# Chunks of 512 tokens from token 6016 on instead of 7424, with the last two transforms in fewer steps and one plain pair instead of two

## The chip, the core and the metric

The kernel runs on one core of one Trainium2 chip. The metric is the device time of one execution in microseconds. The core has five engines that work side by side and wait for each other by semaphores: TensorE (PE in the profile; its weight loads, which overlap the matmuls, are PEld), VectorE (DVE), ScalarE (ACT), GpSimd (POOL) and SyncE (SP), which here only issues DMAs. PE writes its results to PSUM, and DVE and ACT read them from there.

## The reference, cut to what matters

A spectral mixing of `x` (4 batches of 3008 tokens by 256) is followed by a two-layer network of width 2048 over all 12032 tokens.

```python
def _attn_ref(x, w_r, w_i, b_r, b_i):
    X = np.fft.rfft(x, axis=1)
    Yr = Xr @ w_r - Xi @ w_i + b_r
    Yi = Xr @ w_i + Xi @ w_r + b_i
    Yr = np.sign(Yr) * np.maximum(np.abs(Yr) - lam, 0.0)   # lam = 0.01, and the same for Yi
    y = np.fft.irfft(Y, n=x.shape[1], axis=1)

def _moe_ref(x, w_in, w_out, alpha):
    h = x @ w_in
    g = np.maximum(h, 0.0) + alpha * np.minimum(h, 0.0)
    return g @ w_out
```

All is float32. The kernel keeps the accuracy with products of numbers split into a high and a low part: three matmuls (high x high, high x low, low x high) stand for one product.

## The kernel before

**The transforms.** Each batch of 3008 = 47 x 64 tokens goes through these parts. Part a (`a_load`, `a_split`, `a_mm`, `a_evac`) is the first stage of the forward transform, in 16 groups g, whose results are stored to DRAM. Part b (`b_load`, `b_mm`, `b_evac`, `b_evac2`), part m (`m_mm`, `m_mm2`, `m_part`, `m_evac1`: the mixing with `w_r`, `w_i`, the bias and the threshold) and part c (`c_mm`, `c_evac`, with a second store to DRAM) work through 12 slots q; together they are called the middle part here. Part d (`d_load` and `d_step`, or `s_dmm` and `s_dpart`) is the last stage of the inverse transform: each of its 32 runs (dg, 8 to a batch) makes 376 tokens, in PSUM, from which ACT and DVE write the high and low parts `yh`, `yl` that the network reads. The parts take their PSUM tiles from one pool of three, `ps_f`, in the order in which they ask.

**The network.** The tokens go through in chunks. Up to token `T0` a chunk has 384 tokens (256 for chunks 0 and 16), and one *step* is one of the 16 blocks of 128 hidden columns: `l1_step` does 6 matmuls of the first layer into a tile of `ps_h` (two tiles, L680), ACT and DVE make the activation (L686, L687) and split it (L691, L692, the low part on DVE or POOL), and three steps later `l2_step` does the second layer, 9 matmuls of 256 columns (6 in a 256-token chunk; L717 to L719). From `T0` on, a chunk has 512 tokens and one *pair* t of 0 to 7 is two of the 16 blocks: `s_l1` does 12 matmuls of 512 columns (L784), with ACT's L787 and DVE's L788 as activation; `s_sums` makes the operands for the second layer; `s_l2` does that two pairs later. It takes the pair as a 2 x 2 block product, by Winograd's form with seven block products of 3 matmuls (21 matmuls of 256 columns, L884 to L886) where `t` is not in `PLAIN`, and by eight (24 matmuls) where it is. For the form with seven, `s_sums` also makes the differences `t13`, `t24` (t in the profile; L815, L817, L819) and splits them (L820 to L823, the last on POOL); for a plain pair it splits one half-block instead (L806, L808). Both write `dh`, `dl` (L803 with L818 or L807). At the end of a chunk `s_out` (L909 to L919) adds the products up, two pairs into the next chunk, and `s_turn` (L928) transposes the result and stores it, two pairs later, behind `s_sums` of pair 3. The last of the 512-token chunks is done plainly (`z_parts`, L830 and L831, and `z_l2`, L847 to L849: 24 matmuls a pair), with its output written from `zo` tiles.

**The order of the work** is written out by hand. The list of steps has `NS` entries (16 per chunk, 20 chunks, so 320). The functions of the transforms are hung on step numbers with `at(i, fn, ...)`: what stands in `todo` is issued after the matmuls of step i, what stands in `mid` in the middle of it. `AO[b]` is the step at which part a of batch b begins (group g at `AO + 3g//2`), `BO[b]` that of slot 0 of the middle part, and `BP` the number of steps between two slots; slot q of batch 1 is at 49 + 11q//2. Within a slot that begins at step i, m follows at i + 2 and i + 4 and c at i + 8. The d part of a chunk that begins at step i is issued at i - 3. The last 26 steps also make the combined weights of the seven-product form (`w_open`, `w_full`, `w_sums`, `w_split`), in the place of the tables of parts b and c. In the 512-token stage the d parts hang on pairs (`pre`, `post`). Every engine runs its instructions in the order of issue. Most loads and stores are issued from SP's queue, in that order.

The values of the plan that the change touches (L953 to L957):

```python
    AO = {2: 120, 3: 186}
    BO = {2: 154, 3: 222}
    BP = 5
    SLAG = 2
    PLAIN = (1, 2)
```

Of the kernel before, what the change touches and what calls it, by code (L numbers as in the profile page):

```python
# [9 lines left out]
F32 = mybir.dt.float32  # L10
F32R = mybir.dt.float32r
# [4 lines left out]
AF = mybir.ActivationFunctionType  # L16
# [77 lines left out]
def fft_mix_moe(ctx, tc, x, w_r, w_i, b_r, b_i, w_in, w_out, alpha, la, rb, lc, rd, lf, cf, sel, out):  # L94
    nc = tc.nc
    B, S, C = x.shape
    DFF = alpha.shape[0]
    CT = C // 128
    FT = DFF // 128
# [6 lines left out]
    NC = 2 * NCH  # L106
    TC = 384
    assert NC * TC - 128 == NC * TOK

    CC = 20  # L110
    SC = 512

    def head(c):
        return 128 - (TC - TOK) * (c % NC) if c % NC else 0

    def size(c):
        return TC if c % NC else TC - 128

    T0 = (CC // NC) * NC * TOK + TC * (CC % NC) - (128 if CC % NC else 0)
    NS2 = (B * S - T0) // SC  # L120
    assert CC % NC and T0 + SC * NS2 == B * S
    NPAIR = NSLOT // 2

    const = ctx.enter_context(tc.tile_pool(name="const", bufs=1))
    work = ctx.enter_context(tc.tile_pool(name="work", bufs=2))
    dram = ctx.enter_context(tc.tile_pool(name="dram", bufs=4, space=bass.MemoryType.DRAM))
    ps_f = ctx.enter_context(tc.tile_pool(name="ps_f", bufs=3, space=bass.MemoryType.PSUM))
    ps_h = ctx.enter_context(tc.tile_pool(name="ps_h", bufs=2, space=bass.MemoryType.PSUM))
    ps_o = ctx.enter_context(tc.tile_pool(name="ps_o", bufs=2, space=bass.MemoryType.PSUM))

    V, G, A, PE = nc.vector, nc.gpsimd, nc.scalar, nc.tensor

    def f(t):
        return t.bitcast(F32)
# [27 lines left out]
    FH = FT // 2  # L162
    x_s = const.tile([NP, R, C], F32, tag="half0", name="x0")
    a0_s = const.tile([NQ, R // 2, 2, C], F32, tag="half1", name="a0")
    wi_h, wo_h = {}, {}
# [166 lines left out]
    def put(*queues):  # L332
        for n, (o, i) in enumerate(stores):
            (queues or (nc.sync,))[n % max(len(queues), 1)].dma_start(out=o, in_=i)
        stores.clear()

    xt = {}
# [240 lines left out]
    def d_open(c):  # L578
# [3 lines left out]
        if head(c):  # L582
            for t, src in zip((hi, lo), heads.pop(c)):
                if c < CC:
                    t, src = t[:, :, 0:head(c)], f(src)[:, :, 0:head(c)]
# [8 lines left out]
    def d_step(b, g):  # L594
        t = zt.pop((b, g))
        c = NCH * b + g
        assert c < CC
        n0 = (size(c) - head(c)) // CH
# [20 lines left out]
    def s_open(n):  # L619
        yt[CC + n] = [work.tile([128, CT, SC], F32R, tag=tag, name=tag) for tag in ("yh", "yl")]  # L620

    def s_parts(dg):

        s, e = TOK * dg, TOK * dg + TOK
        for n in range((s - T0) // SC, (e - 1 - T0) // SC + 1):
            a, z = max(s, T0 + SC * n), min(e, T0 + SC * (n + 1))
            yield n, (a - s) // CH, (z - s) // CH, a - T0 - SC * n, z - T0 - SC * n

# [6 lines left out]
    def s_dpart(dg, n):  # L635
        parts = []
        for k, n0, n1, a, z in s_parts(dg):
            if k == n:
                for ct in range(CT):
                    ps = ds[dg][ct][:, :, n0:n1]  # L640
                    ys = [y[:, ct] for y in yt[CC + n]]
                    if n == NS2 - 1:
                        hi, lo = (y[:, a:z].rearrange("p (n i) -> p n i", i=CH) for y in ys)
                        parts.append((ps.rearrange("p i n -> p n i"), hi, lo))
                    else:
                        parts.extend(s_dput(ps, ys, a // CH, z // CH))
        for src, hi, lo in parts:
            A.activation(out=hi, in_=src, func=AF.Copy)
        for src, hi, lo in parts:
            V.tensor_tensor(out=lo, in0=src, in1=f(hi), op=ALU.subtract)  # L650
# [84 lines left out]
    PR = FT // 2  # L735
# [37 lines left out]
    sg, sa, sq = {}, {}, {}  # L773

    def s_l1(n, t):
        yh, yl = yt[CC + n]
        q = work.tile([128, 2, SC], F32, tag="xt", name="sq")
        for j in range(2):
            m = 2 * t + j
            ps = ps_h.tile([128, SC], F32, tag="h", name="ps_h")  # L780
            k = 0
            for ct in range(CT):
                for w, a in ((0, yh), (0, yl), (1, yh)):
                    PE.matmul(ps, wi_h[m // FH][:, w, ct, 128 * (m % FH):128 * (m % FH) + 128], a[:, ct],  # L784
                              start=(k == 0), stop=(k == 3 * CT - 1))
                    k += 1
            A.activation(out=q[:, j], in_=ps, func=AF.Relu, scale=-1.0)  # L787
            V.scalar_tensor_tensor(out=q[:, j], in0=q[:, j], scalar=beta_s[:, m:m + 1], in1=ps,  # L788
                                   op0=ALU.mult, op1=ALU.add)
        sq[n, t] = q  # L790

    def s_sums(n, t):
        q = sq.pop((n, t))
        if n == NS2 - 1:
            z_parts(t, q)
            return
# [7 lines left out]
        d = [(dh[:, HS * k:HS * k + HS], dl[:, HS * k:HS * k + HS]) for k in range(3)]  # L804
        if t in PLAIN:
            A.activation(out=h13[:, 0], in_=b12, func=AF.Copy)  # L806
# [19 lines left out]
    def z_parts(t, q):  # L826
        g = []
        for j, tags in enumerate((("xh", "Yh"), ("xl", "Yl"))):
            hi, lo = (work.tile([128, SC], F32R, tag=tag, name="zg") for tag in tags)
            A.activation(out=hi, in_=q[:, j], func=AF.Copy)  # L830
            (V if j else G).tensor_tensor(out=lo, in0=q[:, j], in1=f(hi), op=ALU.subtract)  # L831
            g.append((hi, lo))
        sg[NS2 - 1, t] = g

    def z_l2(t):
        n = NS2 - 1
        if t == 0:
            sa[n] = [ps_f.tile([128, 2, C], F32, tag="f", name="ps_o") for _ in range(2)]
        g = sg.pop((n, t))
        for i in range(4):  # L840
            o = sa[n][i // 2][:, i % 2]
            cols = slice(128 * i, 128 * i + 128)
            for j, (hi, lo) in enumerate(g):
                m = 2 * t + j
                w = wo_h[m // FH][:, m % FH]
                last = m == FT - 1 and i % 2 == 1
                PE.matmul(o, hi[:, cols], w[:, 0], start=(m == 0 and i % 2 == 0), stop=False)  # L847
                PE.matmul(o, hi[:, cols], w[:, 1], start=False, stop=False)
                PE.matmul(o, lo[:, cols], w[:, 0], start=False, stop=last)  # L849
            if t == PR - 1 and i % 2:  # L850
                for k in (i - 1, i):
                    st = work.tile([128, C], F32, tag="gh", name="zo", bufs=4)
                    if k % 2 == 0:
                        A.activation(out=st, in_=sa[n][i // 2][:, 0], func=AF.Copy)
                    else:
                        V.tensor_copy(out=st, in_=o)
                    z_store(T0 + SC * n + 128 * k, st)
                put(nc.sync, nc.scalar)

    def z_store(s0, st):  # L860

        s = s0
        while s < s0 + 128:
            d = s // TOK
            e = min(s0 + 128, (d + 1) * TOK)
            dst = out.rearrange("(b p r) c -> b p r c", b=B, r=R)[d // NCH][:, CH * (d % NCH):CH * (d % NCH) + CH]
            stores.append((dst[(s - d * TOK) // CH:(e - d * TOK) // CH], st[s - s0:e - s0]))
            s = e

    def s_l2(n, t):  # L870
# [16 lines left out]

        if t in PLAIN:
            b11, b22, b21, b12 = sg.pop((n, t))
# [60 lines left out]
    ES = [1, 1, 1, 1, 1, 1, 1, 1, 1, 0, 1, 0, 0, 0, 0, 0]  # L950
    LOS = [0, 1, 0, 0, 1, 1, 0, 1, 1, 0, 1, 1, 0, 1, 0, 0, 1, 1, 0, 0, 1, 0, 1, 1, 1, 1, 1, 0, 1, 1, 0, 1, 1, 0, 1, 1, 0, 1, 1, 0, 1, 1, 0, 1, 1, 0, 1, 1]
    DS = 3
    AO = {2: 120, 3: 186}  # L953
    BO = {2: 154, 3: 222}
    BP = 5
    SLAG = 2
    PLAIN = (1, 2)  # L957
    MP = [3, 4, 4, 4, 4, 5, 5, 6]
    CM = 8
    PB = 49  # L960
# [20 lines left out]
    with tc.manual_schedule():  # L981
# [100 lines left out]
        def at(i, fn, *args, when=todo):  # L1082
            when.setdefault(i, []).append((fn, args))
# [9 lines left out]
        for b in range(B):  # L1093
            s0 = b * per
            for g in range(J if b == 0 else 0, min(NCH, CC - NCH * b)):
                i = s0 + g * FT
# [6 lines left out]
            if b == 0:  # L1103
                for g in range(FILL, NG):
                    i = 6 * (g - FILL) + 9
# [4 lines left out]
            else:  # L1110
                for g in range(NG if b + 1 < B else 0):
                    i = AO[b + 1] + 3 * g // 2
                    if g % 2 == 0:
# [4 lines left out]
            for q in range(NPAIR if b + 1 < B else 0):  # L1118
                i = PB + 11 * q // 2 if b == 0 else BO[b + 1] + BP * q
                at(i - BL, b_load, b + 1, q)  # L1120
# [11 lines left out]
        done = 0  # L1132
        spairs = [(n, t) for n in range(NS2) for t in range(PR)]
        pre, post = {}, {}
        i = NS - 26
# [54 lines left out]
        for k in range(len(spairs) + SLAG):  # L1190
            do(pre, k)
            if k < len(spairs):
                s_l1(*spairs[k])
            do(post, k)
            put()
            if k < SLAG:
                l2(NS - 2 + 2 * k)
            if k == 1:
                do(todo, NS - 1)
            if k >= SLAG:  # L1200
                n, t = spairs[k - SLAG]
                if n == NS2 - 1:
                    z_l2(t)
                else:
                    s_l2(n, t)
                    if t == PR - 1:
                        s_out(n)
            if k < len(spairs):
                s_sums(*spairs[k])
            if k >= SLAG and t == 1 and n:  # L1210
                s_turn(n - 1)
# [33 lines left out]
```

## Time and profile before

| | |
|---|---|
| median of 3 runs | 1384.43 us |
| the runs | 1384.43, 1385.01, 1381.59 us |
| the profiled execution | 1381.03 us, span 1379.1 us, mean granted TensorE clock 0.998 |
| PE busy | 1363.7 us, 99% of the span |
| DVE, ACT, POOL busy | 927.3, 735.7, 398.2 us |
| the 384-token stage, steps 0 to 319 | 107 to 967 us |
| the eight 512-token chunks in the form with seven products | 967 to 1324 us |
| the last chunk of 512 tokens | 1324 to 1374 us |

The span is the time from the first to the last instruction of the profiled execution. Matmuls are pipelined, and their ends in the profile are modelled: one of 256 columns is shown as 0.28 us long, while the next one begins 0.12 us after it. So PE's busy share says little by itself, and lengths are read from start to start.

### The profile page before, as it was taken

How to read it: one execution, taken by the hardware profiler on the slowest of the kernel's cores; microseconds unless marked ns; L12 is line 12 of the kernel's file. 1: busy time of each engine (PE TensorE's matmuls, PEld its weight loads, DVE VectorE, ACT ScalarE, POOL GpSimd, SP SyncE). 2: the span in 40 equal slices, each digit the busy share in tenths (PEclk: the TensorE clock that was granted, in tenths of full speed). 3: DMA queues.
4: the chain of work that ended last, by engine and by line, in shares of the span. 5: the costliest groups of instructions: out<-in, count | busy, mean ns of one | idle time of the engine just before them, and what ended most of it. 6: DMA issues, size and time to landing. Idle time of an engine off the chain costs nothing.

```text
span 1379.1 us, 25262 instructions
## 1 busy us (share of the span) xinstructions
PE 1363.7 (99%) x9550; PEld 1295.2 (94%) x9550; DVE 927.3 (67%) x1689; ACT 735.7 (53%) x1519; POOL 398.2 (29%) x432
## 2 busy tenths in 40 slices
PE   9999999999999999999999999999999999999998
PEld 5979899999999999999999999999999999999997
DVE  2757755666665546676657667666788888888874
ACT  3565655544556645556545454555555555555553
POOL 4855822322322123322222223222112111111121
PEclk9999999999999999999999999999999999999999
DMA  9964222102113311134212111101101110111001
GB/s 239 255 184 148 64 92 73 54 25 62 57 55 107 87 47 54 36 116 132 65 50 62 54 43 58 43 23 36 35 1 39 27 28 5 36 27 28 9 9 31
DMA packets 77700, 89.66 MB, mean 65 GB/s; under 512 B 28829, under 2 KB 60032, under 8 KB 77579
## 3 DMA queue, kind: packets, MB, share of 16 engines
q1 hardware_dynamic: 68993, 76.74, 19.2%
q0 software_dynamic: 5168, 8.02, 2.2%
q10 hardware_dynamic: 3418, 3.29, 0.7%
q8 instruction: 75, 1.23, 0.4%
q14 instruction: 46, 0.38, 0.1%
HBM read 50.49 MB, written 34.34 MB: 62 GB/s over the span
## 4 chain that ended last, share of the span: by engine, by line
PE 92%; DVE 3%; DMA 1%; ACT 1%; issue 1%; POOL 0%; SPq 0%; ACTq 0%; DVEq 0%; POOLq 0%
PE ps_h L680 22%; PE ps_h L784 14%; PE ps_m L486 5%; PE ps_o L718 5%; PE ps_o L719 5%; PE ps_o L717 5%; PE ps_d L611 4%; PE ps_o L885 3%; PE ps_b L426 3%; PE ps_o L886 3%; PE ps_o L884 3%; PE ps_m L473 3%; PE o_last L719 2%; PE o_last L717 2%; PE o_last L718 2%
## 5 line engine op out<-in xcount | busy, mean ns | idle before, releaser
L680 PE MATMUL ps_h<-yh,w 128*128 128x384 f32 (+1 forms) x1216 | 354.1, 334 | 1.3 <-DVE q L687 1.2
L687 DVE SCALAR_TENSOR_TENSOR q<-q,beta_s,ps_h 128x384 f32<-128x384 f32 (+1 forms) x320 | 191.6, 599 | 165.7 <-ACT q L686 162.9
L692 POOL TENSOR_TENSOR gl<-q,gh 128x384 fp32r<-128x384 f32 (+1 forms) x155 | 160.8, 1038 | 462.0 <-ACT gh L691 410.1
L691 ACT ACTIVATE gh<-q 128x384 fp32r<-128x384 f32 (+1 forms) x320 | 164.7, 515 | 238.9 <-DVE q L687 236.1
L680 PEld LDWEIGHTS ps_h<-yh,w 128*128 128x128 f32 x1216 | 223.1, 189 | 4.2 <-issue 1.3
L680 PE MATMUL ps_h<-yl,w 128*128 128x384 f32 (+1 forms) x608 | 200.4, 330 | 0.0
L686 ACT ACTIVATE q<-ps_h 128x384 f32<-128x384 f32 (+1 forms) x320 | 151.5, 473 | 82.7 <-PE ps_h L680 64.5
L784 PE MATMUL ps_h<-yh,w 128*128 128x512 f32 x576 | 191.3, 393 | 0.0
L719 PE MATMUL ps_o<-w,gl 128*128 128x256 f32 x640 | 180.4, 282 | 3.3 <-POOL gl L692 3.3
L718 PE MATMUL ps_o<-w,gh 128*128 128x256 f32 x640 | 180.6, 282 | 0.0
L717 PE MATMUL ps_o<-w,gh 128*128 128x256 f32 x640 | 180.0, 281 | 0.0
L823 POOL TENSOR_TENSOR l<-t,h 128x512 fp32r<-128x512 f32 x48 | 62.2, 1296 | 296.7 <-ACT h L821 283.1
L692 DVE TENSOR_TENSOR gl<-q,gh 128x384 fp32r<-128x384 f32 (+1 forms) x165 | 101.5, 615 | 49.9 <-ACT gh L691 47.9
L784 PEld LDWEIGHTS ps_h<-yh,w 128*128 128x128 f32 x576 | 108.2, 188 | 21.3
L788 DVE SCALAR_TENSOR_TENSOR sq<-sq,beta_s,ps_h 128x512 f32<-128x512 f32 x144 | 103.2, 742 | 36.1 <-ACT sq L787 35.9
L719 PEld LDWEIGHTS ps_o<-w,gl 128*128 128x128 f32 x640 | 121.6, 190 | 4.2 <-POOL gl L692 4.1
L718 PEld LDWEIGHTS ps_o<-w,gh 128*128 128x128 f32 x640 | 121.5, 190 | 0.1
L717 PEld LDWEIGHTS ps_o<-w,gh 128*128 128x128 f32 x640 | 120.6, 188 | 0.1
L680 PEld LDWEIGHTS ps_h<-yl,w 128*128 128x128 f32 x608 | 114.8, 189 | 1.4
L784 PE MATMUL ps_h<-yl,w 128*128 128x512 f32 x288 | 112.9, 392 | 0.0
L787 ACT ACTIVATE sq<-ps_h 128x512 f32<-128x512 f32 x144 | 82.3, 593 | 34.1 <-PE ps_h L784 33.4
L803 ACT ACTIVATE dh<-sq 128x768 fp32r<-128x768 f32 x64 | 54.1, 846 | 72.1 <-DVE sq L788 37.9
(211 smaller groups left out, 3145.2 us busy)
## 6 DMA issues: line engine op xcount, KB each, us to landing
zt<-zd SPq DMA_DIRECT2D x32, 384.0 KB
ad<-ast SPq DMA_DIRECT2D x48, 192.0 KB
bt<-ad SPq DMA_DIRECT2D x72, 128.0 KB
zd<-zst SPq DMA_DIRECT2D x36, 256.0 KB
xt<-in_x SPq DMA_DIRECT2D x21, 320.0 KB
cw_s<-in_moe_w_in SPq DMA_DIRECT2D x8, 512.0 KB
cw_s<-in_moe_w_out SPq DMA_DIRECT2D x8, 512.0 KB
bt<-a POOLq DMA_DIRECT2D x24, 128.0 KB, 7.7
```

The costliest lines, as they stand in the source:

```text
L486: PE.matmul(p, a[:, k:k + 128], mix[i][:, w, ct], start=(n == 0), stop=(n == 3 * CT - 1))
L680: PE.matmul(ps, wi_h[m // FH][:, w, ct, 128 * (m % FH):128 * (m % FH) + 128], a[:, ct, 0:n], start=(k == 0), stop=(k == 3 * CT - 1))
L686: A.activation(out=q, in_=ps, func=AF.Relu, scale=-1.0)
L687: V.scalar_tensor_tensor(out=q, in0=q, scalar=beta_s[:, m:m + 1], in1=ps, op0=ALU.mult, op1=ALU.add)
L691: A.activation(out=hi, in_=q, func=AF.Copy)
L692: (V if LOS[(2 * m + c) % len(LOS)] and fill or not fill and (m + c) % 2 else G).tensor_tensor(out=lo, in0=q, in1=f(hi), op=ALU.subtract)
L717: PE.matmul(a, hi[:, t], w[:, 0], start=(i, k) in first, stop=False)
L718: PE.matmul(a, hi[:, t], w[:, 1], start=False, stop=False)
L719: PE.matmul(a, lo[:, t], w[:, 0], start=False, stop=(i, k) in last)
L784: PE.matmul(ps, wi_h[m // FH][:, w, ct, 128 * (m % FH):128 * (m % FH) + 128], a[:, ct], start=(k == 0), stop=(k == 3 * CT - 1))
L787: A.activation(out=q[:, j], in_=ps, func=AF.Relu, scale=-1.0)
L788: V.scalar_tensor_tensor(out=q[:, j], in0=q[:, j], scalar=beta_s[:, m:m + 1], in1=ps, op0=ALU.mult, op1=ALU.add)
```

## The change

The switch to chunks of 512 tokens is moved from chunk 20 (token 7424) to chunk 16 (token 6016, where the third batch begins): `CC` is 16 instead of 20. The list of steps shrinks from 320 to 256, and the 6016 remaining tokens are cut into eleven chunks of 512 and a last one of 384, which `ZC` and the slices let the last chunk's functions handle. The step numbers of the transforms of batches 2 and 3 move forward, the slots of their middle part come every 4 steps instead of every 5, and of the eight pairs of a 512-token chunk only pair 1 stays plain.

```diff
-    CC = 20
+    CC = 16
     SC = 512
...
-    NS2 = (B * S - T0) // SC
-    assert CC % NC and T0 + SC * NS2 == B * S
+    NS2 = -(-(B * S - T0) // SC)
+    ZC = B * S - T0 - SC * (NS2 - 1)
...
-        for n in range((s - T0) // SC, (e - 1 - T0) // SC + 1):
+        for n in range(max(s - T0, 0) // SC, (e - 1 - T0) // SC + 1):
...
     def s_l1(n, t):
         yh, yl = yt[CC + n]
-        q = work.tile([128, 2, SC], F32, tag="xt", name="sq")
+        w1 = SC if n < NS2 - 1 else ZC
+        q = work.tile([128, 2, SC], F32, tag="xt", name="sq")[:, :, 0:w1]
...
-            hi, lo = (work.tile([128, SC], F32R, tag=tag, name="zg") for tag in tags)
+            hi, lo = (work.tile([128, SC], F32R, tag=tag, name="zg")[:, 0:ZC] for tag in tags)
...
-        for i in range(4):
+        for i in range(ZC // 128):
+            end = i % 2 == 1 or i == ZC // 128 - 1
...
-            if t == PR - 1 and i % 2:
-                for k in (i - 1, i):
+            if t == PR - 1 and end:
+                for k in range(i - i % 2, i + 1):
...
-    AO = {2: 120, 3: 186}
-    BO = {2: 154, 3: 222}
-    BP = 5
+    AO = {2: 92, 3: 146}
+    BO = {2: 126, 3: 176}
+    BP = 4
     SLAG = 2
-    PLAIN = (1, 2)
+    PLAIN = (1,)
```

## Rows read from the trace of the kernel before

**Rows 1.** The page: span, then busy us, share and instructions of engines.

```profile
span 1379.1 us, 25262 instructions
...
PE 1363.7 (99%) x9550; PEld 1295.2 (94%) x9550; DVE 927.3 (67%) x1689; ACT 735.7 (53%) x1519; POOL 398.2 (29%) x432
```

**Rows 2.** The page: shares of engines in the chain that ended last.

```profile
PE 92%; DVE 3%; DMA 1%; ACT 1%; issue 1%; POOL 0%; SPq 0%; ACTq 0%; DVEq 0%; POOLq 0%
```

**Rows 3.** Busy time by stretch; the first line names the columns.

```profile
core 0: us, PE busy (x) PEld busy (x) DVE busy (x) ACT busy (x) POOL busy (x), PEclk, DMA share, GB/s
...
589.00:674.00 85.00, 83.70 (x595) 80.64 (x595) 58.65 (x108) 50.01 (x107) 23.41 (x25) 1.00 0.36 109
...
811.00:851.00 40.00, 39.83 (x330) 39.08 (x330) 28.06 (x60) 20.22 (x52) 12.27 (x17) 1.00 0.19 60
...
967.00:1324.00 357.00, 357.00 (x2305) 325.54 (x2304) 291.03 (x546) 201.20 (x391) 61.94 (x48) 1.00 0.09 24
```

**Rows 4.** PE's waits, 160 to 967 us: us in total, times, longest.

```profile
PE ps_d L611 <- ACT ast L404: 0.8, 1, 0.8
PE ps_a L390 <- DVE hl L142: 0.5, 1, 0.5
```

**Rows 5.** Timeline of PE (start, length): first matmuls of two bare 384-token steps.

```profile
479.00 0.34 PE L680 MATMUL ps_h<-yh,w 128*128 128x384 f32 x1
...
481.12 0.34 PE L680 MATMUL ps_h<-yh,w 128*128 128x384 f32 x1
```

**Rows 6.** Timeline of PE: two steps of the 256-token chunk begin.

```profile
828.22 0.36 PE L680 MATMUL ps_h<-yh,w 128*128 128x256 f32 x1
...
829.74 0.28 PE L680 MATMUL ps_h<-yh,w 128*128 128x256 f32 x1
829.86 0.28 PE L680 MATMUL ps_h<-yl,w 128*128 128x256 f32 x1
```

**Rows 7.** Timeline of PE: pairs 0, 1, 4 and 5 of one chunk begin.

```profile
1009.58 0.40 PE L784 MATMUL ps_h<-yh,w 128*128 128x512 f32 x1
...
1014.81 0.40 PE L784 MATMUL ps_h<-yh,w 128*128 128x512 f32 x1
...
1030.88 0.39 PE L784 MATMUL ps_h<-yh,w 128*128 128x512 f32 x1
...
1036.50 0.39 PE L784 MATMUL ps_h<-yh,w 128*128 128x512 f32 x1
```

**Rows 8.** DVE's groups, 967 to 1324 us: busy, mean ns | idle before.

```profile
L815 DVE TENSOR_TENSOR t<-sq 128x512 f32<-128x512 f32 x48 | 33.1, 690 | 1.4
L822 DVE TENSOR_TENSOR l<-t,h 128x512 fp32r<-128x512 f32 x47 | 32.2, 685 | 0.0
L817 DVE TENSOR_TENSOR t<-sq,t 128x256 f32<-128x256 f32 x48 | 20.4, 425 | 5.1 <-DVE t L815 0.5
...
L808 DVE TENSOR_TENSOR l<-sq,h 128x256 fp32r<-128x256 f32 x16 | 6.7, 418 | 0.0
```

**Rows 9.** Timeline of ACT and DVE in pair 4 of the same chunk.

```profile
1030.96 0.85 ACT L803 ACTIVATE dh<-sq 128x768 fp32r<-128x768 f32 x1 [2.15 <-PE o_last L885]
...
1033.66 1.42 DVE L928 STREAM_TRANSPOSE oT<-c 128x256 f32<-128x256 f32 x4
...
1035.00 0.70 DVE L788 SCALAR_TENSOR_TENSOR sq<-sq,beta_s,ps_h 128x512 f32<-128x512 f32 x1
```

**Rows 10.** Timeline of POOL in that pair; DVE's group in the last chunk.

```profile
1033.94 1.30 POOL L823 TENSOR_TENSOR l<-t,h 128x512 fp32r<-128x512 f32 x1 [14.85 <-ACT h L821]
...
L831 DVE TENSOR_TENSOR zg<-sq,zg 128x512 fp32r<-128x512 f32 x8 | 10.0, 1244 | 13.9 <-ACT zg L830 13.9
```

**Rows 11.** Timeline of DVE at the end.

```profile
1375.33 0.42 DVE L856 COPY zo<-ps_o 128x256 f32<-128x256 f32 x1 [1.76 <-ACT zo L854]
```

More of the change, by code (lines that the diff above doesn't have):

```diff
@@ L776, in s_l1 @@
         yh, yl = yt[CC + n]
-        q = work.tile([128, 2, SC], F32, tag="xt", name="sq")
+        w1 = SC if n < NS2 - 1 else ZC
+        q = work.tile([128, 2, SC], F32, tag="xt", name="sq")[:, :, 0:w1]
         for j in range(2):
             m = 2 * t + j
-            ps = ps_h.tile([128, SC], F32, tag="h", name="ps_h")
+            ps = ps_h.tile([128, SC], F32, tag="h", name="ps_h")[:, 0:w1]
             k = 0
@@ L783, in s_l1 @@
                 for w, a in ((0, yh), (0, yl), (1, yh)):
-                    PE.matmul(ps, wi_h[m // FH][:, w, ct, 128 * (m % FH):128 * (m % FH) + 128], a[:, ct],
+                    PE.matmul(ps, wi_h[m // FH][:, w, ct, 128 * (m % FH):128 * (m % FH) + 128], a[:, ct, 0:w1],
                               start=(k == 0), stop=(k == 3 * CT - 1))
@@ L845, in z_l2 @@
                 w = wo_h[m // FH][:, m % FH]
-                last = m == FT - 1 and i % 2 == 1
+                last = m == FT - 1 and end
                 PE.matmul(o, hi[:, cols], w[:, 0], start=(m == 0 and i % 2 == 0), stop=False)
@@ L849, in z_l2 @@
                 PE.matmul(o, lo[:, cols], w[:, 0], start=False, stop=last)
-            if t == PR - 1 and i % 2:
-                for k in (i - 1, i):
+            if t == PR - 1 and end:
+                for k in range(i - i % 2, i + 1):
                     st = work.tile([128, C], F32, tag="gh", name="zo", bufs=4)
                     if k % 2 == 0:
-                        A.activation(out=st, in_=sa[n][i // 2][:, 0], func=AF.Copy)
+                        A.activation(out=st, in_=sa[n][k // 2][:, 0], func=AF.Copy)
                     else:
-                        V.tensor_copy(out=st, in_=o)
+                        V.tensor_copy(out=st, in_=sa[n][k // 2][:, 1])
                     z_store(T0 + SC * n + 128 * k, st)
```

## Prediction

> **What bounds the kernel now.** I read the page first: TensorE (PE) is busy 1363.7 of 1379.1 us, VectorE (DVE) 927.3 [rows 1], and 92% of the chain that ended last is PE [rows 2]. Both are averages, so the table by stretch comes next [rows 3]. In the stage of 512-token chunks (967 to 1324 us) PE is busy all of its 357.00 us and DVE 291.03, or 82%. Where the transform of batch 3's input runs beside the middle of batch 2's (589 to 674), PE lacks 1.30 us of 85.00; around the 256-token chunk (811 to 851) it lacks 0.17 of 40.00. Busy time flatters a pipelined engine, so PE's waits are read too: from 160 to 967 us the two longest are 0.8 and 0.5 us [rows 4]. So from 160 us on the time is the number of matmuls times their spacing, and a change is worth what it does to that sum, as long as the other engines keep up.
>
> **Fewer and cheaper matmuls.** The length of a step is the distance between the first L680 matmuls of two steps, which counts spacing and not modelled ends. A bare step of a 384-token chunk takes 481.12 - 479.00 = 2.12 us [rows 5]. A step of the 256-token chunk has 12 matmuls spaced 0.12, so 1.44 us; the one shown took 1.52 [rows 6]. I take 1.44, the work alone, and keep 1.52 for the range. A pair of a 512-token chunk takes 1014.81 - 1009.58 = 5.23 us where the second layer is the seven-product form, and 1036.50 - 1030.88 = 5.62 where it is plain [rows 7]; a pair of the last chunk holds the same number of matmuls as a plain one, so 5.62 too.
>
> The tokens from 6016 on cost before: 16 x 1.44 (chunk of 256) = 23.0; 48 x 2.12 (three of 384) = 101.8; eight chunks of 6 x 5.23 + 2 x 5.62 = 42.62, so 341.0; the last chunk 8 x 5.62 = 45.0. Sum 510.7. After: eleven chunks of 7 x 5.23 + 5.62 = 42.23, so 464.5; the last chunk has 384 tokens, whose pair holds the matmuls of two 384-token steps, 16 x 2.12 = 33.9. Sum 498.5. Saved on PE: **12.3 us** (13.5 with 1.52). Of this the second plain pair gives 0.39 a chunk. The transforms' own matmuls (a, b, m, c, d) stay the same in number; they only move.
>
> **What the seventh product form adds.** Pair 2 gets on DVE one 512-wide difference (0.690), two 256-wide ones (0.425 each) and a 512-wide remainder in place of a 256-wide (0.685 - 0.418): 1.81 us a chunk [rows 8]. ScalarE, busy 201.20 of the 357.00 us, gets two wider conversions, and GpSimd (POOL) one subtraction of 1.30 [rows 3, 10]. On a path or beside it? DVE idles 66.0 us in the 357, which hold eight chunks [rows 3], so 8.2 us a chunk: there is room in total. The tight place is where the work is late. The buffer ps_h holds two tiles, so the L784 matmuls of the next pair start only when DVE's L788 has read the tile two before. At pair 4 of a chunk (it starts at 1030.88), L788 starts late, at 1035.00, behind the four transposes of s_turn, and takes 0.70; the next pair begins at 1036.50 [rows 7, 9]. Slack 0.80 us. After the change the plain second layer leaves this pair, so it ends 0.39 earlier: **slack 0.41**. L788 itself does not move: the chain ahead of it begins with dl, which waits for dh, and the buffer of dh is freed by the last products of pair 1's plain second layer, at the start of pair 4 (dh is written from 1030.96) [rows 9], before as after. Pair 3 has the longer 5.62 us, and the added 1.8 us goes into the wait for that buffer. So I cost it at nothing; if the cover is gone, each chunk pays what exceeds 0.41 us, eleven times.
>
> **The transforms in fewer steps.** Batches 2 and 3 must now be through within 256 steps instead of 320. Input transforms (a) overlapped the middle part (b, m, c) only once, for 24 steps; now they do so for batch 2 (steps 92 to 114, beside batch 1's middle part, 49 to 117) and batch 3 (146 to 168 beside 126 to 178), some 48 steps. The middle part comes every 4 steps instead of 5. All of them and d_step draw on three ps_f tiles in order: the two waits of [rows 4] are of that kind. The overlap cost 1.30 us [rows 3]; twice that is 2.6, so +1.3, against which the 0.17 of the 256-token chunk falls away. Ends: -1.5 (all of it gone) and +8 (each of the nine d_steps from step 93 to 221 finds a full 0.8 us wait like the one shown). I take **+1.0**, near the row of the same kind of overlap. At DVE 58.65 of 85.00 us in that stretch [rows 3] I see no engine taking over there.
>
> **Queues and waits moved.** SyncE's (SP) queue gets the loads of batches 2 and 3 earlier and more of the transposed stores (11 chunks of them instead of 8); the DMA share of the 512-token stage is 0.09 [rows 3], and the loads there are issued three pairs (15.7 us) ahead. The first load of batch 3's middle part follows the last input-transform store by 4 steps instead of 10, and stands in SP's queue till that has landed; it is needed 4 steps (some 12 us) after its issue. No row of before shows so short a distance. Bounds: 0, since PE waits for no load after 160 us, and some 5 us once, if the load is late by two steps. I take 0. The preparation of the combined weights keeps its 26 steps and now follows batch 3's last step at once (228, 230): 0.
>
> **The end.** Before, two evacuations close the last block, ScalarE's and after it a DVE copy of 0.42 us [rows 11]; with three blocks of 128 the last has no partner: **-0.4**.
>
> **The sum** is made against the profiled execution, 1381.03 us (its span 1379.1 and 1.9 around it): 12.3 + 0.4 - 1.0 = 11.7, so 1369.3. The three timed runs have their median at 1384.43, one of them near the profiled one (1381.59); from the median it is 1372.7. Halfway between: **1371 us**.
>
> **Rivals.** (1) DVE is a little late in the 512-token stage: the 0.41 us of slack is used up, and 0.3 to 0.6 us a chunk show as PE idle, 3 to 7 us in all: 1374 to 1378. For it: the slack is small, and it shrinks because PE gets faster. Against: the wait for dh sets when pair 4's work begins.
> (2) The transforms are crowded: the upper bound of +8 instead of +1, or a late load once: 1376 to 1379. For it: four ps_f tiles (m1, c, b, a) are now asked for within one step, at steps 146, 150, 158 and 162, and d, d, b, a at 93; before, this happened at step 189 alone. Against: PE lost only 1.30 us in the overlap of before.
> (3) Slower: DVE and POOL collide. The last chunk shows it: its 128x512 subtraction on DVE takes 1.244 us on the mean beside POOL's, where the same shape in the 512-token stage takes 0.685 [rows 8, 10], so 0.56 each time. POOL's new subtraction comes in pair 3. If it falls on the difference or the remainder there, and nothing of the new work is absorbed, a chunk loses 1.81 + 0.56 - 0.41 = 1.96 us, eleven chunks 21.6: 1371 + 21.6 = 1393. It turns the sign from a lateness of 1.5 us a chunk (0.41 + 11.7/11). Against: POOL's subtraction runs from 1033.94 for 1.30 us [rows 10], while DVE reads PSUM (L788 from 1035.00) or transposes one input; the two-input work lies before and after it, and the new pair repeats that order.
> The Trainium skill states the rule behind it ("SBUF - State Buffer", section "Who interferes with whom"): a DVE instruction with two SBUF inputs contends with a GpSimd instruction that reads SBUF, and the one that comes second waits for the whole of the first. By that rule a badly placed collision would cost up to 1.30 us and not 0.56, so 1401 us; the rows of the last chunk agree with the kind, and those of the 512-token stage show none.
>
> **Chances.** Forecast (1368 to 1374) 0.70; rival 1 0.12; rival 2 0.10; rival 3 0.04; the rest 0.04, split between better (all bounds good: 13.5 + 0.4 + 1.5 = 15.4 saved) and a mixture of 1 and 2 that ends at no change. The range runs from 1367 (15.4 off the mean of the two starting points, 1382.7) to 1379, the end of rivals 1 and 2. About 0.3%, some 4 us, is what a measurement of this kernel can tell from no change. Faster by more than that (below 1380.3): 0.88; within: 0.07; slower: 0.05.
>
> **What would show it.** In the profile after, the pairs of 512-token chunks must be 5.23 us, seven times, and 5.62 once; pair 4 shows 5.23 if the slack holds and more if rival 1 is right. PE busy falls by some 12 us, and PE's waits between 160 us and the 512-token stage stay below 4 us. If DVE's t, l or su take over 1 us in that stage, it is rival 3; if PE waits for ScalarE or DVE on ps_d, ps_a, ps_b by more than 5 us in all, rival 2. The prediction fails if a pair's length is no longer set by its matmuls.

## The result: 1370.66 us, and the profile after

| | median | runs | against the kernel before |
|---|---|---|---|
| before | 1383.01 us | 4 (1381.58 to 1385.01) | |
| after | 1370.66 us | 4 (1370.02 to 1371.94) | 0.9915 [0.9903, 0.9927] |

The change saves 12.35 us on the medians; the interval of the ratio gives 10.1 to 13.4. The forecast was 1371 us, from a sum of 11.7 us saved.

The page after: the span, and busy us of the engines.

```profile
span 1368.7 us, 25199 instructions
...
PE 1352.7 (99%) x9367; PEld 1274.7 (93%) x9367; DVE 993.1 (73%) x1821; ACT 749.5 (55%) x1528; POOL 400.1 (29%) x421
```

Against [rows 1]: 183 matmuls fewer and PE's busy time 11.0 us shorter, and DVE's 65.8 us longer. DVE was given much more to do, and the time fell all the same. Busy time by stretch, columns as in [rows 3]; here 836 to 1324 us is the stage of the eleven 512-token chunks:

```profile
208.00:836.00 628.00, 626.48 (x4599) 618.07 (x4598) 422.63 (x788) 336.31 (x717) 169.83 (x200) 1.00 0.22 69
836.00:1324.00 488.00, 488.00 (x3148) 444.67 (x3147) 418.59 (x790) 283.85 (x551) 99.63 (x77) 1.00 0.09 24
```

PE is busy for all of the 488.00 us again, while DVE has gone from 82% [rows 3] to 418.59/488.00 = 86%. The lengths of the pairs, from the timeline of PE: the beginnings of pairs 4, 5 and 6 of one chunk, and of two pairs of the last chunk, which now has 384 tokens.

```profile
990.08 0.39 PE L785 MATMUL ps_h<-yh,w 128*128 128x512 f32 x1
...
995.30 0.40 PE L785 MATMUL ps_h<-yh,w 128*128 128x512 f32 x1
...
1000.53 0.40 PE L785 MATMUL ps_h<-yh,w 128*128 128x512 f32 x1
...
1342.17 0.34 PE L785 MATMUL ps_h<-yh,w 128*128 128x384 f32 x1
...
1346.41 0.34 PE L785 MATMUL ps_h<-yh,w 128*128 128x384 f32 x1
```

Pair 4 takes 5.22 us where it took 5.62 [rows 7], pair 5 takes 5.23, and a pair of the last chunk 4.24, twice the 2.12 of [rows 5]. These are the lengths that the sum was made with. The timeline of DVE in the same pair 4 (L788 of before is L789 here):

```profile
992.85 1.42 DVE L930 STREAM_TRANSPOSE oT<-c 128x256 f32<-128x256 f32 x4
...
994.19 0.70 DVE L789 SCALAR_TENSOR_TENSOR sq<-sq,beta_s,ps_h 128x512 f32<-128x512 f32 x1
```

The activation ends at 994.89, and the next pair begins at 995.30: slack 0.41 us, where it was 0.80 [rows 9]. The prediction had worked out 0.41.

PE's waits between 208 and 840 us (in total, times, longest), to be held against [rows 4]:

```profile
PE ps_a L390 <- ACT Xh L440: 0.7, 1, 0.7
PE ps_h L680 <- DVE q L687: 0.3, 1, 0.3
PE ps_a L390 <- ACT zst L561: 0.2, 1, 0.2
PE ps_a L390 <- DVE hl L142: 0.2, 1, 0.2
```

In all 1.4 us, as little as before. Waits count only from the modelled end of a matmul. Counted from start to start (the distance to the next matmul less what is usual for the form: 229 ns for 512 columns, 174.5 for 384, 119.2 for 256, 112 for 128, 110 for 94), PE loses 4.45 us from step 48 to the last step of the stage, against 4.11 in the kernel before.

From the two traces, start to start: from step 48 to the first 512-token pair 758.66 us became 627.33, and from there to the last matmul 407.06 became 526.78, together 11.61 us less. The rest of the span is 0.15 us longer at the end and 1.06 us longer ahead of step 48, where the two programs are the same (in the traces of the experiments step 48 begins anywhere from 207.4 to 210.3 us, so this part scatters by more).

### The profile page after: what moved, and what is told of

Read it like the earlier page. It is cut to its first block, busy times and chain, and to the rows that moved or that the text cites. A ratio compares the mean times of both kernels' runs of the same rounds, so it can differ in the third digit from the quotient of the medians.

```text
span 1368.7 us, 25199 instructions
## 1 busy us (share of the span) xinstructions
PE 1352.7 (99%) x9367; PEld 1274.7 (93%) x9367; DVE 993.1 (73%) x1821; ACT 749.5 (55%) x1528; POOL 400.1 (29%) x421
## 4 chain that ended last, share of the span: by engine, by line
PE 92%; DVE 3%; ACT 2%; issue 1%; DMA 1%; POOL 0%; ACTq 0%; SPq 0%; DVEq 0%; POOLq 0%
PE ps_h L785 19%; PE ps_h L680 17%; PE ps_m L486 5%; PE ps_o L887 4%; PE ps_o L888 4%; PE ps_o L886 4%; PE ps_o L719 4%; PE ps_o L718 4%; PE ps_o L717 4%; PE ps_d L611 4%; PE ps_b L426 3%; PE ps_m L473 3%; PE o_last L719 2%; PE o_last L717 2%; PE o_last L718 2%; PE ps_a L387 2%
## 5 line engine op out<-in xcount | busy, mean ns | idle before, releaser
L680 PE MATMUL ps_h<-yh,w 128*128 128x384 f32 (+1 forms) x960 | 282.8, 336 | 1.6 <-DVE q L687 1.5
L785 PE MATMUL ps_h<-yh,w 128*128 128x512 f32 (+1 forms) x768 | 251.7, 388 | 0.0
L824 POOL TENSOR_TENSOR l<-t,h 128x512 fp32r<-128x512 f32 x77 | 99.9, 1297 | 389.8 <-ACT h L822 357.6
L789 DVE SCALAR_TENSOR_TENSOR sq<-sq,beta_s,ps_h 128x512 f32<-128x512 f32 (+1 forms) x192 | 133.9, 731 | 44.3 <-ACT sq L788 43.4
L680 PE MATMUL ps_h<-yl,w 128*128 128x384 f32 (+1 forms) x480 | 159.2, 332 | 0.0
L785 PE MATMUL ps_h<-yl,w 128*128 128x512 f32 (+1 forms) x384 | 148.6, 387 | 0.0
L718 PE MATMUL ps_o<-w,gh 128*128 128x256 f32 x512 | 144.6, 282 | 0.0
L717 PE MATMUL ps_o<-w,gh 128*128 128x256 f32 x512 | 144.1, 282 | 0.0
L788 ACT ACTIVATE sq<-ps_h 128x512 f32<-128x512 f32 (+1 forms) x192 | 106.3, 585 | 23.2 <-PE ps_h L785 22.4
L718 PEld LDWEIGHTS ps_o<-w,gh 128*128 128x128 f32 x512 | 97.3, 190 | 0.1
L717 PEld LDWEIGHTS ps_o<-w,gh 128*128 128x128 f32 x512 | 96.5, 188 | 0.1
L822 ACT ACTIVATE h<-t 128x512 fp32r<-128x512 f32 x77 | 48.7, 633 | 82.1 <-DVE t L820 79.9
```

Of the source, the lines that this page charges most:

```text
L717: PE.matmul(a, hi[:, t], w[:, 0], start=(i, k) in first, stop=False)
L718: PE.matmul(a, hi[:, t], w[:, 1], start=False, stop=False)
L824: G.tensor_tensor(out=l24, in0=t24, in1=f(h24), op=ALU.subtract)
```

## Experiments

All ratios are against the kernel before, run on the same chip beside them. The theory was that PE's matmul sum decides the time wherever DVE's work keeps its slack, and that the slack, not DVE's total, is what can run out.

**1. One part alone.** The changed kernel with two plain pairs again:

```diff
-    PLAIN = (1,)
+    PLAIN = (1, 2)
```

> The changed kernel with pairs 1 and 2 plain again, all else as changed. Theory (the time is the sum of matmul spacings as long as VectorE's work keeps its slack): pair 4 of each of the eleven 512-token chunks goes back from 5.23 to 5.62 us, 11 x 0.39 = 4.3 us more than the changed kernel, so about 1375.0. Rival (VectorE is already late in the changed kernel, so the plain pair costs PE nothing that it does not wait for anyway): 1370 to 1372.

1374.23 us, 0.9944 [0.9930, 0.9959]; the pairs 4 are 5.62 us again with a slack of 0.80. And the kernel before with only its plain pair taken:

```diff
-    PLAIN = (1, 2)
+    PLAIN = (1,)
```

> The kernel before with only pair 1 plain, chunks and steps as before. Theory: eight 512-token chunks lose 0.39 us each, 3.1 us less than before, about 1380; pair 4 becomes 5.23 us and its slack falls from 0.80 to 0.41 us. What is left of the gain, some 8 to 9 us, is then due to the chunks and the moved transforms. Rival (the seventh product form is paid back on VectorE): 1383, as before.

1378.54 us, 0.9975 [0.9965, 0.9985], that is 3.3 us less than the 1381.84 of the kernel before beside it. In the traces the 512-token stage gets 4.22 us longer by the first edit (526.78 to 531.00, start to start) and 3.11 us shorter by the second (407.06 to 403.95). So the plain pair is worth 3 to 4 us of the 12, in both directions what its matmuls weigh (4.3 and 3.1). That the chunks and transforms bring the rest follows by subtraction; no run changes them alone.

**2. The same work in another order.** Pair 2 plain in place of pair 1, everything else as changed:

```diff
-    PLAIN = (1,)
+    PLAIN = (2,)
```

> The changed kernel with pair 2 plain in place of pair 1: the same matmuls, the same work on VectorE, in another order. Theory of the slack: pair 1 now has the longer operand work directly behind the eight additions of s_out; the activation of pair 2's first block, which today ends 0.66 us before it is needed, comes about 2.2 us later, so each of eleven chunks stalls by 1.3 to 2 us: 1385 to 1393. Rival (only the totals count: VectorE idles 8 us a chunk): 1370 to 1372.

1389.59 us, 1.0055 [1.0040, 1.0070]: slower than the kernel before, by the order alone. PE's waits in the 512-token stage, and the timeline of one chunk, where pair 2 begins at 982.42 (DVE, ACT and PE):

```profile
PE ps_h L785 <- DVE sq L789: 17.0, 10, 1.7
...
984.72 0.41 DVE L921 TENSOR_TENSOR c<-su 128x256 f32<-128x256 f32 x1
985.05 0.68 DVE L816 TENSOR_TENSOR t<-sq 128x512 f32<-128x512 f32 x1
985.83 0.42 DVE L818 TENSOR_TENSOR t<-sq,t 128x256 f32<-128x256 f32 x1
986.18 0.95 DVE L819 TENSOR_TENSOR dl<-sq,dh 128x768 fp32r<-128x768 f32 x1
987.04 0.42 DVE L820 TENSOR_TENSOR t<-sq,t 128x256 f32<-128x256 f32 x1
987.38 0.68 DVE L823 TENSOR_TENSOR l<-t,h 128x512 fp32r<-128x512 f32 x1
988.71 1.40 DVE L789 SCALAR_TENSOR_TENSOR sq<-sq,beta_s,ps_h 128x512 f32<-128x512 f32 x2 [0.64 <-ACT sq L788]
...
987.56 0.63 ACT L822 ACTIVATE h<-t 128x512 fp32r<-128x512 f32 x1 [1.10 <-DVE t L820]
988.10 1.06 ACT L788 ACTIVATE sq<-ps_h 128x512 f32<-128x512 f32 x2
...
989.51 0.50 PE L785 MATMUL ps_h<-yh,w 128*128 128x512 f32 x1 [1.70 <-DVE sq L789]
```

The chain is to be read upwards: PE waits for L789, that for ACT's L788, that stands in ACT's queue behind L822, which waits for DVE's second difference L820, which follows the eight additions of s_out (the last is L921). Once a chunk (ten of them) that is 1.7 us of waiting; start to start pair 2 takes 7.09 us (982.42 to 989.51) where it takes 5.23 in the changed kernel. A rule by totals, with VectorE some 6 us a chunk idle, cannot see this.

**3. No plain pair.** Pair 1 in the seven-product form too; `s_out` then needs one evacuation and one addition less:

```diff
-    PLAIN = (1,)
+    PLAIN = ()
...
-        A.activation(out=e[2], in_=o_last[:, 1], func=AF.Copy)
...
-        V.tensor_tensor(out=u[1], in0=e[2], in1=e[1], op=ALU.subtract)
...
-        V.tensor_tensor(out=c2[:, 0], in0=u[3], in1=u[1], op=ALU.add)
+        V.tensor_tensor(out=c2[:, 0], in0=u[3], in1=e[1], op=ALU.subtract)
```

> The changed kernel with no plain pair at all; s_out then needs one evacuation and one addition less. Sum of matmuls alone: 11 x 0.39 = 4.3 us less, 1366.4. Theory of the slack: the added 1.8 us behind s_out are not covered (0.66 us of slack in pair 2), and with no plain pair ahead of it the transposes of s_turn find no cover either; 2 to 3.5 us of stall a chunk against 0.39 saved: 1388 to 1405, the gain turns into a loss.

1386.64 us, 1.0033 [1.0016, 1.0050]. The loss is a little below the range expected: PE waits 15.3 us in all for L789, nearly all of it at pair 2, 1.5 us at a time, while the transposes of `s_turn`, for which a second stall was expected, cost only 0.2 to 0.4 us, in the six chunks whose pair 4 has them and no d part beside them. The direction stands: the last plain pair is no reserve, it is the cover for `s_out`.

**4. The collision of rival 3, brought about.** DVE's remainder `l13` moved to GpSimd, where it runs beside `dl` and the second difference:

```diff
-        V.tensor_tensor(out=l13, in0=t13, in1=f(h13), op=ALU.subtract)
+        G.tensor_tensor(out=l13, in0=t13, in1=f(h13), op=ALU.subtract)
```

> The changed kernel with VectorE's remainder l13 (0.685 us a pair) done on GpSimd, where it runs beside VectorE's two-input subtraction dl. Rival 3 of the prediction put to the test: each collision should lengthen dl from 0.95 us by about 0.5, and VectorE wins 0.685 for it. If the collision costs no more than that, the pairs stay at 5.23 us and the time at 1369 to 1373; if whole instructions block each other (1.30 us each), lateness of more than 0.41 us reaches PE in pairs 2 to 5 and the time is above 1380.

1428.69 us, 1.0332 [1.0311, 1.0353]: 0.685 us a pair taken from DVE, and 58 us lost against the changed kernel. The groups of the 512-token stage (busy us, mean ns), and one place in the timeline:

```profile
L820 DVE TENSOR_TENSOR t<-sq,t 128x256 f32<-128x256 f32 x76 | 115.1, 1514 | 0.0
...
L823 POOL TENSOR_TENSOR l<-t,h 128x512 fp32r<-128x512 f32 x76 | 127.4, 1676 | 234.9 <-ACT h L821 234.9
...
1013.64 0.95 DVE L819 TENSOR_TENSOR dl<-sq,dh 128x768 fp32r<-128x768 f32 x1
1014.50 1.51 DVE L820 TENSOR_TENSOR t<-sq,t 128x256 f32<-128x256 f32 x1
...
1014.06 1.67 POOL L823 TENSOR_TENSOR l<-t,h 128x512 fp32r<-128x512 f32 x1 [2.18 <-ACT h L821]
```

It is not `dl` that is lengthened, as I had expected: it began first and takes its 0.95 us, and GpSimd waits for it (1.67 us where it takes 1.30 alone, [rows 10]). The next two-input instruction of DVE, L820, then waits for GpSimd, 1.51 us instead of 0.42. So the collision costs DVE 1.09 us a pair, all of it ahead of the activation, twice what the prediction had put on it (0.56). In the chunks without a d part in pair 4, pairs 1, 4 and 5 take 6.2 us instead of 5.2.
The Trainium skill's rule ("SBUF - State Buffer", section "Who interferes with whom"), that the one that comes second waits for the whole of the first, agrees with this trace: L820 ends 0.28 us after GpSimd's instruction, at 1016.01 and 1015.73.

**5. VectorE's real reserve.** GpSimd's subtraction `l24` on DVE instead, with no collision but 0.685 us more a pair:

```diff
-        G.tensor_tensor(out=l24, in0=t24, in1=f(h24), op=ALU.subtract)
+        V.tensor_tensor(out=l24, in0=t24, in1=f(h24), op=ALU.subtract)
```

> The changed kernel with GpSimd's subtraction of each seven-product pair done on VectorE instead (0.685 us a pair, 4.8 us a chunk). If totals decide: VectorE idles about 6 us a chunk in the changed kernel, so nothing changes, 1370.7. Theory of the slack: VectorE's spare time in a pair is the 0.66 us in which its first activation waits for ScalarE, and the new work fills it and 0.2 us more; the loop of a pair gets longer than PE's 5.23 us by about 0.2, so pairs stretch once the slack is used, 8 to 20 us in all: 1378 to 1391.

1373.81 us, 0.9935 [0.9915, 0.9955], 3 us more than the changed kernel. The theory had the kind right and the size wrong (8 to 20 us were expected): the new work (L824) does go into the 0.66 us in which DVE waits for ACT, as the timeline shows (the activation L789 behind it waits no more), and only pair 4, the one with the least slack, stretches, from 5.22 to 5.67 us (pair 5 behind it by 0.1), in the six chunks whose pair 4 has the transposes and is not lengthened by a d part. A rule by totals (1370.7 expected) was not met either.

```profile
971.60 0.69 DVE L824 TENSOR_TENSOR l<-t,h 128x512 fp32r<-128x512 f32 x1 [0.18 <-ACT h L822]
972.21 1.40 DVE L789 SCALAR_TENSOR_TENSOR sq<-sq,beta_s,ps_h 128x512 f32<-128x512 f32 x2
```

**6. More slack for pair 4, which PE should not notice.** The operands that the second layer needs only two pairs later (`h13`, `h24`, `dl`, `l13`, `l24`) are issued behind the next pair's activation. In `s_sums` the second difference moves ahead, and the rest becomes a function called after `s_l1`:

```diff
-        V.tensor_tensor(out=dl, in0=q[:, HS:], in1=f(dh), op=ALU.subtract)
         V.tensor_tensor(out=t24[:, 1], in0=b21, in1=t24[:, 0], op=ALU.subtract)
+        s_rest.append((n, t, q, dh, dl, d, t13, t24, h13, l13, h24, l24))
+
+    s_rest = []
+
+    def s_late():
+        if not s_rest:
+            return
+        n, t, q, dh, dl, d, t13, t24, h13, l13, h24, l24 = s_rest.pop()
+        V.tensor_tensor(out=dl, in0=q[:, HS:], in1=f(dh), op=ALU.subtract)
         A.activation(out=h13, in_=t13, func=AF.Copy)
...
                 s_l1(*spairs[k])
+            s_late()
             do(post, k)
```

Once with no plain pair, and once with pair 1 plain:

> No plain pair, as in the run without one, but the work of a pair that the second layer needs only two pairs later (the high parts h13 and h24, the remainders dl, l13 and l24) is issued behind the next pair's activation instead of ahead of it. Theory of the slack: what stalled was the order, an activation behind ScalarE's h24, which waits for VectorE's t24; with that gone VectorE needs about 42.4 us of a chunk's 43.8, every pair takes 5.23 us and the 4.3 us of the plain pairs are won: 1366 (1365 to 1368). Rival (VectorE's total is the bound without a plain pair): stalls of 1 us or more a chunk stay, 1377 or more.

> The changed kernel (pair 1 plain) with the same later issue of the operands. Theory: PE already ran without a stall in the 512-token stage, so more slack for VectorE is worth nothing there: 1370 to 1371.5, with the slack in pairs 4 and 5 well above the 0.4 and 0.5 us of the changed kernel. Rival (VectorE's lateness costs the changed kernel time that the pair lengths do not show): 2 us or more faster.

1392.00 us (1.0074 [1.0061, 1.0087]) and 1388.70 us (1.0043 [1.0027, 1.0058]); both miss what was expected. The groups of the second, 836 to 1340 us, and PE's waits there:

```profile
L828 DVE TENSOR_TENSOR dl<-sq,dh 128x768 fp32r<-128x768 f32 x75 | 101.8, 1357 | 0.0
L831 DVE TENSOR_TENSOR l<-t,h 128x512 fp32r<-128x512 f32 x75 | 87.3, 1164 | 0.0
...
PE ps_o L894 <- DVE c L927: 6.0, 10, 0.7
PE ps_h L785 <- DVE sq L789: 4.9, 10, 0.5
```

`dl` takes 1.357 us on the mean instead of 0.953, and `l13` 1.164 instead of 0.685: in the new order GpSimd's subtraction begins ahead of `dl` in 42 of the 75 pairs and ahead of `l13` in the other 33. That is the collision of experiment 4 again, some 0.9 us a pair, and I had left it out. The new order also puts this work ahead of `s_out`, so that PE waits for the second layer's PSUM tiles (L927 is the addition that frees them). Nearly all of the second run's loss lies there: pair 2 takes 6.7 to 7.0 us in ten chunks where it took 5.23, pair 3 0.1 us more, and pairs 4 to 7 keep their lengths. The slack of pair 4, which was to grow, fell to 0.35. How much of the loss is the collision and how much the order was not separated.

The time of the first run lies in the range of its rival (1377 or more), by which DVE's total is the bound without a plain pair. Its busy time by stretch, columns as before:

```profile
836.00:1339.00 503.00, 485.04 (x3076) 436.37 (x3075) 485.06 (x803) 293.84 (x545) 115.88 (x87) 1.00 0.09 23
```

DVE is busy for 485.06 of 503.00 us, the collisions' lengthening included, so this rival is not excluded. Whether the order helps without GpSimd's instruction in its way was not shown; the two runs do not carry the theory.

**7. Crowding the transforms.** The slots of the middle part every 3 steps instead of 4:

```diff
-    BP = 4
+    BP = 3
```

> The changed kernel with the slots of the middle part every 3 steps instead of 4 (batches 2 and 3): the same work of the transforms crowded further, the steps after it empty. Theory (PE's matmul sum decides, the other engines have room; VectorE about 75 to 80% busy in those steps instead of 66 to 79%): PE's waits in the transforms change by no more than some 2 us, 1369 to 1373. Rival (crowding the three ps_f tiles and the in-order queues costs, and the changed kernel already pays for it): 4 to 10 us more, 1375 to 1381.

1367.26 us, 0.9886 [0.9870, 0.9903]: **3.4 us faster** than the changed kernel and below both expected ranges, by crowding the work. The interval meets the changed kernel's (0.9903 to 0.9927) at its edge; the traces agree with it, as the stretch from step 48 to the first 512-token pair falls from 627.33 to 624.59 us. Busy time from 440 to 610 us, first the changed kernel, then this one:

```profile
440.00:610.00 170.00, 168.67 (x1225) 163.65 (x1225) 119.42 (x222) 92.85 (x199) 47.04 (x56) 1.00 0.27 83
```

```profile
440.00:610.00 170.00, 170.00 (x1252) 167.14 (x1251) 118.21 (x227) 95.43 (x204) 46.80 (x56) 1.00 0.29 89
```

PE's idle 1.33 us are gone. Counted from start to start, the loss after step 48 falls from 4.45 to 1.72 us. In steps 144 to 175, where batch 3's part a runs beside the middle part, it falls from 3.62 to 0.07; steps 192 to 207 lose 0.73 us more.

**8. Was it the coincidence?** With slots every 4 steps, m's third part, c and b ask for PSUM tiles in the same step; with 3 they never do. Part c one step later, slots every 4:

```diff
-    CM = 8
+    CM = 9
```

> The changed kernel with part c nine steps after its slot's begin instead of eight, slots still every 4 steps. In the changed kernel the third part of m, then c and b ask for their PSUM tiles in the same step and part a joins them four times; with slots every 3 steps this never happens, and 2.7 us of PE's stalls in the transforms went. If the coincidence is the cause, c one step later takes most of them away here too, with the slots as dense as before: 1367 to 1369, and PE's stalls between steps 144 and 175 fall from 3.6 to about 1 us. If it is something else about the denser slots (a shorter stretch beside part a), nothing changes: 1370 to 1371.

1370.52 us, 0.9920 [0.9906, 0.9935], as the changed kernel. The loss of steps 144 to 159 falls from 1.50 to 0.49 us, but that of 160 to 175 stays (2.12, now 2.18) and that of steps 96 to 111 grows from 0.48 to 1.30. PE's waits from 208 to 840 us show other ones in their place:

```profile
PE ps_m L486 <- ACT ast L404: 1.1, 1, 1.1
PE ps_m L486 <- DVE Yc L524: 0.8, 1, 0.8
```

So the coincidence named is a part of it at most; which alignment of a, m, c, b and d costs the rest stays open.

**9. One overlap instead of two.** Slots every 3 steps, and part a of batch 2 behind batch 1's middle part:

```diff
-    AO = {2: 92, 3: 146}
-    BO = {2: 126, 3: 176}
-    BP = 4
+    AO = {2: 114, 3: 150}
+    BO = {2: 142, 3: 182}
+    BP = 3
```

> Slots every 3 steps as in that run, with part a of batch 2 moved behind the middle part of batch 1 (steps 114 to 136, middle parts from 142 and 182, part a of batch 3 from 150), so that only batch 3's overlaps. By the term of the prediction the overlap of part a with batch 1's middle part costs about 1 us (PE's stalls of steps 80 to 111): 1366 to 1367 against 1367.3. If the overlap costs nothing, 1367.3.

1367.19 us, 0.9898 [0.9881, 0.9914]: no difference in time that could be measured from experiment 7. In the trace the loss of steps 80 to 111 falls from 0.96 to 0.02 us, while steps 112 to 143 lose 0.56 us more, so the overlap with batch 1 cost about 1 us where it lay, and half of that is lost again where part a went.

## Why the prediction was right, step by step

| step | predicted | what the traces showed |
|---|---|---|
| matmuls saved | 12.3 us | pair and step lengths as put in; 11.6 us from step 48 to the last matmul, with the 0.34 lost in the transforms in it, so some 11.9 |
| slack of pair 4 | 0.80 to 0.41, no stall | 0.41, and PE busy for all of 488.00 us |
| transforms | +1.0 (-1.5 to +8) | +0.34, start to start |
| a late load of batch 3 | 0 (to 5) | 0: no loss in steps 176 to 191 |
| the end | -0.4 | +0.15 |
| sum | 11.7 | 12.35 on the medians; 10.4 between the two spans, with 1.06 of that lost ahead of step 48 |

**What bounds the kernel** was read rightly: the two runs of experiment 1 give the matmuls' price back where the slack holds, and experiment 2 shows that the same matmuls take 1.9 us a chunk longer where it does not.

**The number** owes something to luck. The transforms came out 0.66 us better than put in and the end 0.55 us worse, and the two cancel. The same sum gives 1369.3 or 1372.7 from the two starting points of the prediction; that halfway between them is within 0.4 us of the median shows no such accuracy. The chances do not agree with each other: the forecast and rivals 1 and 2, 0.92 together, all lie below 1380.3 us, on which 0.88 was put. And the bound of +8 us was loose: nine waits of 0.8 us are 7.2.

**The slack** was the step on which the sign hung, and it came out to the hundredth, because the wait that sets it (for the buffer of `dh`) is the same in both kernels. The wait itself shrank. In pair 4 of before (it starts at 1030.88) and, below it, of the changed kernel (990.08):

```profile
1031.85 0.96 DVE L818 TENSOR_TENSOR dl<-sq,dh 128x768 fp32r<-128x768 f32 x1 [1.00 <-ACT dh L803]
```

```profile
990.16 0.85 ACT L804 ACTIVATE dh<-sq 128x768 fp32r<-128x768 f32 x1 [1.54 <-PE o_last L887]
...
991.04 0.96 DVE L819 TENSOR_TENSOR dl<-sq,dh 128x768 fp32r<-128x768 f32 x1 [0.21 <-ACT dh L804]
```

`dl` begins 0.97 and 0.96 us after the pair, but of the 1.00 us that DVE waited, 0.21 is left. With the slack of 0.41 that is all the reserve of the step that the prediction priced at nothing. Nor would every chunk have paid, as it said: the 0.41 stands in six of the eleven chunks. The first chunk has no transposes (slack 0.98), and in four a d part stretches pair 4 to 6.93 us (slack over 2). That the room in DVE's total says nothing was argued with one row; experiment 2 shows it.

**The transforms** were mis-sized, and their mechanism only half seen. The +1.0 stood for twice the overlap. Start to start the one overlap before cost 1.97 us (steps 176 to 207) and not the 1.30 of the busy time; the two overlaps after cost 0.96 (with batch 1, where experiment 9 finds it) and 3.62. Against that, 0.68 us in steps 112 to 143 and the 1.1 us in the 256-token chunk's steps went away, of which the busy time had shown only 0.17. Rival 2 saw a danger in density. Experiment 7 shows that denser slots lose 2.7 us less here. That the alignment of the slots is the cause was not shown: experiment 8 leaves it open.

**The end** failed: the sign was wrong. The last evacuation has no partner now, but it follows the one before it by so little that it meets the issue of that one's store in ACT's own queue. The timeline of ACT at the end, of before and then of the changed kernel:

```profile
1373.61 1.26 ACTq L334 DMA_DIRECT2D out<-zo  x1
1374.92 0.38 ACT L854 ACTIVATE zo<-ps_o 128x256 f32<-128x256 f32 x1 [1.80 <-PE ps_o L849]
```

```profile
1362.91 0.38 ACT L856 ACTIVATE zo<-ps_o 128x256 f32<-128x256 f32 x1 [3.14 <-PE ps_o L851]
1363.32 1.52 ACTq L334 DMA_DIRECT2D out<-zo  x1
1364.89 0.38 ACT L856 ACTIVATE zo<-ps_o 128x256 f32<-128x256 f32 x1 [1.59 <-issue]
```

The last matmul begins at 1363.31, and ACT comes to the last block only at 1364.89, after 1.52 us of issuing a DMA. Before, an issue stood in ACT's way as well (1.26 us), but the matmuls of two blocks ran beside it, and now those of one. So ACT came to its block 1.07 us after the last matmul's beginning (1373.85), and now 1.58 us after it. The DVE copy that fell away, 0.42 us [rows 11], was paid back there.

**Rival 3** had the right place and too low a price: the collision costs 1.09 us where it happens (experiment 4) and not 0.56, because the last chunk's mean, from which the 0.56 came, is of instructions that began when GpSimd was partly done (0.48 us into its subtraction in six of the eight). It did not happen here, since the new pair repeats an order that keeps the two apart: from 836 to 1324 us none of GpSimd's subtractions overlaps one of DVE with both inputs in SBUF, and DVE's keep their lengths (busy us, mean ns):

```profile
L823 DVE TENSOR_TENSOR l<-t,h 128x512 fp32r<-128x512 f32 x76 | 52.0, 685 | 0.0
...
L820 DVE TENSOR_TENSOR t<-sq,t 128x256 f32<-128x256 f32 x76 | 31.8, 419 | 0.0
```

## What to carry to other kernels

Where one engine is busy without a gap, price a change by that engine's start-to-start distances, and ask of every other engine not how busy it is but how long before its deadline each result comes: 86% busy with 0.41 us to spare was free, and the same load in another order cost 19 us. A pair or step that looks like a leftover of the slower form may be the cover for work that comes once a round; find out what is issued behind it before taking it away. When parts of different periods share a few buffers, try another period: here packing them more densely took stalls away.

## What was not expected of the hardware

- A two-input subtraction on DVE and one on GpSimd did not share: DVE's 0.42 us became 1.51, GpSimd's 1.30 became 1.67, and 0.685 us taken from DVE's list made the kernel 58 us slower.
- A DMA issued from ACT's queue held ACT for 1.52 us, at the one place where nothing else was left to cover it; in the kernel before it was 1.26 us there.
